# One set of five sigmoid buffers, V in three single-buffered tiles, one buffer for raw K, and four more weight tiles loaded during attention

## The chip, the cores and the metric

The kernel runs on one core of a Trainium2 chip. The metric is the device time of one execution in microseconds, the median of several runs. A core has a matrix engine (PE, whose weight loads are shown apart as PEld), a vector engine (DVE), an activation engine (ACT), a general engine (POOL) and a queue engine (SP); here SP issues every transfer. Transfers move between DRAM and the on-chip SBUF; matmuls write to PSUM. Each engine works through its own instructions in order and waits on semaphores that the others raise.

## The reference

Attention with a sigmoid in place of the softmax, and a "soft" mixture of experts on its output. Shapes: 8 batches, 12 heads, 448 positions, head size 64; 8 experts of 4 slots, model size 768, hidden size 1024.

```
scores = scale * q @ k.T - log(S)
attn   = sigmoid(scores);  x = attn @ v            # per batch and head
x      -> (3584, 768)
logits = x @ phi                                   # (3584, 32 slots)
slot_input = softmax over tokens(logits).T @ x     # (32, 768)
slot_out[e] = relu(slot_input[e] @ w1[e]) @ w2[e]  # per expert
out    = softmax over slots(logits) @ slot_out     # (3584, 768)
```

All inputs are float32. The weights w1 and w2 are 50 MB, q, k and v 33 MB, the output 11 MB.

## The kernel before, in words

The kernel has two stages that share the SBUF one after the other.

**Attention.** Two heads make a pair (128 partitions), and a loop takes two pairs, `pa` and `pb`, in each of 24 iterations (`NG`, three iterations to a batch). K's 448 positions are cut in three full chunks of 128 and a rest of 64, the "mid" chunk. One iteration issues on PE, in this order: `qk_full(pa)` and `qk_full(pb)` (scores, three chunks each), `av_full(pa)`, `av_full(pb)` (the product with V), the gate's `logits` of the iteration before, `qk_mid(n + 1)` (the mid scores of the next iteration) and `av_mid(n)`. ACT turns every chunk's scores into a sigmoid tile (`sigmoid`), six full ones and one mid per iteration. DVE copies the result out of PSUM (`evac`), transposes it (`turn`), and makes from the raw Q and K of the next two pairs the split float32r tiles `qs` and `ks` that `qk_full` reads (`split_all`, four DVE instructions per pair). SP loads Q and K of the next two pairs (`load_qk`), V of the next iteration (`load_v`), and a few weight units (`load_unit`).

From the fourth iteration on, the three iterations of a batch carry the gate's work for the batch before, and the code names them `edge` (n % 3 = 0), `after` (1) and `third` (2):

- edge: last logits between the two `av_full`, then `logits_add`, `softmax_a` and `softmax_b`.
- after: `softmax_r`, `softmax_c` and `spread`, which writes a tile to DRAM and reads it back four times (`zd`, `dr`); then, behind the splits, `logits` into PSUM buffer 3, `combine_b`, `logits_add`, and on PE `slot_job` ahead of `qk_mid`, which takes PSUM buffer 3 again.
- third: `slot_evac`, four `turn`s, `combine_c`; its `logits` are in PSUM buffer 0, which the next iteration's `qk_full` takes first.

The order on PE, SP, DVE and ACT is the order of the program's text (`manual_schedule`); semaphores come from the tiles: a new tile in a buffer waits until all readers of the old one are through. PSUM has four double buffers, `bank2(0)` to `bank2(3)`.

**Weights.** w1 and w2 are cut in 128 units of [128, 768] (384 KB). They go through a ring of `N_A + N_B` = 68 tiles: 47 `wa` tiles exist from the start and are filled during attention (`weights_of`: 3, 3, 3 units, then 4, 0, 3 per batch), and 21 `wb` tiles lie over the memory of the attention tiles and are filled as those come free, at the end of attention. Every later unit goes into the ring's next tile when its old unit has been used. The pools lie in SBUF in the order in which they are opened, and `wb0`, `wb1`, ... from the first attention pool upwards.

**Experts and output.** After the last softmax (`last_job`), `w1_part` and `w2_step` run through the units, and `out_batch` makes the output in 16 pieces of four stores each. The last 16 units (`N_LATE`) are mixed with the first 16 stores. Tiles of the output take places in the same ring.

## Time and profile before

| what | value |
|---|---|
| median of 3 runs | 391.66 us (391.07 to 392.79) |
| the profiled execution | 390.38 us, of which the span is 388.6 us |
| PE busy | 365.3 us, 94% of the span |
| DVE / ACT busy | 226.1 us (58%) / 187.5 us (48%) |
| bytes moved | 97.52 MB, mean 251 GB/s |
| attention | until about 283 us, then experts and output |

The profile cuts the span in 40 slices; a digit is the busy share of an engine in that slice in tenths. The view by stage gives the busy time of each engine between two times. The chain of waits follows the work that ended last back from its end: each step says which instruction or transfer held the next one. A name such as `PE b L182` is an engine, the tile that it writes and the line of the kernel; `SPq` is the queue engine issuing a transfer, `out<-in` its target and source. In the timeline, the first number of a row is its start and the second its duration; `[1.55 <-PE b L218]` is the idle time ahead of it and who ended it.

### The profile page before, as it was taken

The page shows a single profiled execution, that of the slowest core. Times are in us where ns is not written, and L with a number is a line of the kernel's source. Part 1 is how long each engine was busy: PE and PEld are TensorE (multiplying, and loading weights), DVE is VectorE, ACT ScalarE, POOL GpSimd, SP SyncE. Part 2 cuts the span into 40 slices and gives each one's busy share as a digit, 9 for nine tenths or more (in the row PEclk, how much of TensorE's full clock was granted, in tenths as well). Part 3 has the DMA queues.
Part 4 walks back from the last instruction along what each step waited for, and adds up shares of the span by engine and source line. Part 5 has one row for each costly group of instructions (what it writes and reads, how often), then busy time and mean ns, then how long its engine had stood idle before and what let it go on. Part 6 is the DMA issues. An engine that isn't in the chain of part 4 may idle for free.

```text
span 388.6 us, 9551 instructions
## 1 busy us (share of the span) xinstructions
PE 365.3 (94%) x3994; PEld 189.8 (49%) x3994; DVE 226.1 (58%) x518; ACT 187.5 (48%) x243; POOL 3.3 (1%) x13
## 2 busy tenths in 40 slices
PE   8999999999999999999999999999989989978760
PEld 7444556554555654555554455554455543224220
DVE  3655677775887677697767777776543410430250
ACT  5655676564567556566635666564531110320240
POOL 1000000000000000000000000000020000000000
PEclk9999999999999999999999999999999999999995
DMA  7766855662784567476446654323999999999997
GB/s 228 260 240 236 300 171 183 237 252 83 265 295 138 178 229 255 135 257 240 177 140 228 238 164 156 143 101 98 292 406 400 400 400 400 398 407 399 373 302 231
DMA packets 42363, 97.52 MB, mean 251 GB/s; under 512 B 4816, under 2 KB 16720, under 8 KB 42320
## 3 DMA queue, kind: packets, MB, share of 16 engines
q1 hardware_dynamic: 42320, 96.91, 70.3%
q8 instruction: 31, 0.51, 0.5%
q14 instruction: 12, 0.10, 0.1%
HBM read 85.43 MB, written 11.47 MB: 249 GB/s over the span
## 4 chain that ended last, share of the span: by engine, by line
PE 80%; DMA 14%; DVE 1%; SPq 1%; ACT 1%; issue 0%; ACTq 0%
PE b L189 29%; PE b L171 24%; DMA wa<-in_w_dram 8%; PE b L182 6%; DMA wb<-in_w_dram 6%; PE b L198 5%; PE b L312 4%; PE px L522 4%; PE b L218 3%; PE b L407 1%; PE px L565 1%; PE px L539 1%; SPq L579 1%; DMA out_dram<-wa 1%; DVE wa L570 0%
## 5 line engine op out<-in xcount | busy, mean ns | idle before, releaser
L161 ACT ACTIVATE att<-b,nbias 128x896 f32<-128x896 f32 x144 | 131.9, 1015 | 12.0 <-PE b L171 12.0
L189 PE MATMUL b<-att,v 128*64 128x448 f32 x576 | 115.3, 545 | 0.0
L171 PE MATMUL b<-qs,ks 64*128 64x448 f32 x864 | 95.9, 372 | 0.0
L171 PEld LDWEIGHTS b<-qs,ks 64*128 64x128 f32 x864 | 77.4, 184 | 26.6 <-PE b L182 11.3
L189 PEld LDWEIGHTS b<-att,v 128*64 128x64 f32 x576 | 38.5, 136 | 61.6 <-issue 50.2
L161 ACT ACTIVATE attm<-b,nbias 128x896 f32<-128x896 f32 x24 | 24.2, 1008 | 70.4 <-PE b L182 70.4
L207 DVE COPY xT<-b 128x896 f32<-128x896 f32 x23 | 25.1, 1092 | 32.7 <-PE b L198 32.7
L152 DVE TENSOR_TENSOR qs<-qkt,qs 128x448 fp32r<-128x448 f32 x48 | 30.0, 625 | 1.7
L152 DVE TENSOR_TENSOR ks<-qkt,ks 128x384 fp32r<-128x384 f32 x48 | 26.8, 558 | 1.6
L213 DVE STREAM_TRANSPOSE y<-xT 128x448 f32<-128x448 f32 x48 | 27.3, 617 | 0.4
L182 PE MATMUL b<-qkt 64*64 64x448 f32 x192 | 24.1, 570 | 0.0
L150 DVE CAST qs<-qkt 128x448 fp32r<-128x448 f32 x48 | 18.2, 380 | 8.8 <-DMA qkt<-in_qk_dram 7.7
L198 PE MATMUL b<-attm,v 64*64 64x448 f32 x192 | 22.4, 537 | 0.0
L570 DVE COPY wa<-px 96x768 f32<-96x768 f32 x13 | 12.2, 952 | 13.7 <-PE px L565 12.9
L570 ACT COPY wa<-px 128x768 f32<-128x768 f32 x13 | 10.3, 799 | 18.1 <-PE px L565 14.2
L565 PE MATMUL px<-st,lt_all 32*128 32x384 f32 (+1 forms) x128 | 16.7, 524 | 1.5 <-DVE st L601 0.7
L312 PE MATMUL b<-y,dr 32*32 32x192 f32 x896 | 17.7, 331 | 0.2 <-ACT dr L303 0.2
L218 PEld LDWEIGHTS b<-xT,phit 128*32 128x32 f32 x384 | 9.1, 109 | 17.0 <-issue 13.4
L522 PE MATMUL px<-wa,sT 128*32 128x256 f32 x282 | 16.8, 381 | 0.6 <-DVE sT L380 0.6
L150 DVE CAST ks<-qkt 128x384 fp32r<-128x384 f32 x47 | 16.6, 353 | 0.0
L218 PE MATMUL b<-xT,phit 128*32 128x96 f32 (+1 forms) x384 | 16.0, 266 | 0.2
L601 DVE COPY st<-px 128x384 f32<-128x384 f32 x2 | 1.1, 557 | 25.3 <-PE px L599 25.3
(132 smaller groups left out, 229.3 us busy)
## 6 DMA issues: line engine op xcount, KB each, us to landing
wa<-in_w_dram SPq DMA_DIRECT2D x92, 384.0 KB, 7.7
qkt<-in_qk_dram SPq DMA_DIRECT2D x48, 448.0 KB, 3.8
wb<-in_w_dram SPq DMA_DIRECT2D x36, 384.0 KB, 5.7
v<-in_v_dram SPq DMA_DIRECT2D x24, 448.0 KB, 5.7
out_dram<-wa SPq DMA_DIRECT2D x26, 192.0 KB, 3.3
out_dram<-wa SPq DMA_DIRECT2D x26, 144.0 KB, 3.3
dr<-zd SPq DMA_DIRECT2D x28, 64.0 KB, 2.0
out_dram<-wb SPq DMA_DIRECT2D x6, 192.0 KB, 5.5
```

The source lines that it names most:

```text
L150: copy(dst[:, 0, :], src)
L152: nc.vector.tensor_tensor(out=dst[:, 1, :], in0=src, in1=dst[:, 0, :].bitcast(F32), op=ALU.subtract)
L161: nc.scalar.activation(att[:], sc[:, :, 0:S], AF.Sigmoid, bias=nbias, scale=QSCALE)
L171: nc.tensor.matmul(sc[:, h, 0:S], ks[r, z, c * P:(c + 1) * P], qs[r, y, :], start=(z + y == 0), stop=(z == 1))
L182: nc.tensor.matmul(sc[r, h, 0:S], t[d, S + NQK:QW], t[d, 0:S], start=True, stop=True)
L189: nc.tensor.matmul(avs["p", p][r, 0:S], vs[n][:, i * (NFULL + 1) + c, r], atts[p, c][:, h, :], start=(start and c == 0), stop=(stop and c ...
L198: nc.tensor.matmul(avs["p", 2 * n + i][d, 0:S], vt[r, NFULL, d], att[r, h, :], start=start, stop=stop)
L207: nc.vector.tensor_copy(xTs[n][:], avs[n][:, :, 0:S])
L213: nc.vector.transpose(ys[b][:, hp, :], xTs["p", p])
L218: nc.tensor.matmul(lp[32 * j:32 * j + 32, 0:TOK[j]], phi_sb[:, p % NPR, :], xTs["p", p][:, TOF[j]:TOF[j] + TOK[j]], start=(first and m == ...
L312: nc.tensor.matmul(sl[a // 2][32 * j:32 * j + 32, a % 2, 0:NPR * BLK], drs[b][32 * a:32 * a + 32, j, c * BLK:(c + 1) * BLK], y[32 * a:32 * ...
L522: nc.tensor.matmul(ph[32 * j:32 * j + 32, uu, 0:256], sT[:, 3 * kh + kc, :], utile[("w1", e, 2 * uu + j // 2, kh)][:, kc * 256:(kc + 1) * ...
```

## The change

- The seven sigmoid tiles become five (`homes`): within an iteration the fifth and sixth sigmoid write over the first and second, the next mid one over the third, and the roles rotate from iteration to iteration.
- V of an iteration, before one tile in two buffers, becomes three tiles with one buffer each: `v0` and `v1` (the full chunks of pair a and of pair b) and `v2` (the mid chunks). `v0` and `v1` for the next iteration are loaded behind the weights; `v1` for a third iteration and every `v2` are loaded in the iteration that uses them.
- The load of Q and K is cut in two: Q with the mid K (`qkt`, two buffers, as before) and the full chunks of K (`kf`), for which there is one buffer for both pairs. The load for `pb + 2` comes behind `split_all(pa + 2)` in the program. Pair 1 alone uses the last weight tile's place. On the host the mid K is put ahead of the full K.
- In edge iterations the K part of `split_all(pb + 2)` goes behind `softmax_b`, and the logits there take PSUM buffer 3 in place of 0.
- Weight units are issued behind `split_all(pa + 2)` and the second K load in place of ahead of `qk_full(pa)`. 51 `wa` tiles and 17 `wb` tiles make the ring of 68.

```diff
@@ -25,12 +25,12 @@
 NFC = F // P
 HALF = DM // 2
 UNIT = 768
-N_A = 47
-N_B = 21
+N_A = 51
+N_B = 17
 N_LATE = 16
 N_MIX = 4
-NATT = 5
 QW = 2 * S
+QM = QW - NQK
 NP = B * NPR
 NG = B * NQ
 WARM = 8
@@ -116,9 +116,9 @@
     with ExitStack() as actx:
         ldq = actx.enter_context(tc.tile_pool(name="ldq", bufs=2))
         sp = actx.enter_context(tc.tile_pool(name="sp", bufs=2))
-        ata = actx.enter_context(tc.tile_pool(name="ata", bufs=1))
-        atb = actx.enter_context(tc.tile_pool(name="atb", bufs=1))
-        lvp = actx.enter_context(tc.tile_pool(name="lvp", bufs=2))
+        one = {}
+        for name in ("kf", "v0", "att4", "att3", "v2", "att0", "att1", "att2", "v1"):
+            one[name] = actx.enter_context(tc.tile_pool(name=f"{name}p", bufs=1))
         yp = actx.enter_context(tc.tile_pool(name="yp", bufs=1))
         xp = actx.enter_context(tc.tile_pool(name="xp", bufs=1))
         bounce = actx.enter_context(tc.tile_pool(name="bounce", bufs=2, space=bass.MemoryType.DRAM))
@@ -127,39 +127,47 @@
         def bank2(i):
             return ps.tile([P, 2, 512], F32, name=f"b{i}")
 
-        qkts, vs, splits, atts, avs, xTs, ys, dts, drs = {}, {}, {}, {}, {}, {}, {}, {}, {}
-
-        def load_qk(p):
+        kfs, qkts, vs, splits, atts, avs, xTs, ys, dts, drs = {}, {}, {}, {}, {}, {}, {}, {}, {}, {}
+
+        def load_qk(p, part=None):
             if p < NP:
-                t = ldq.tile([P, QW], F32, name="qkt")
-                nc.sync.dma_start(t[:], qk[p])
-                qkts[p] = t
-
-        def load_v(n):
+                if part != 1:
+                    qkts[p] = ldq.tile([P, QM], F32, name="qkt")
+                    nc.sync.dma_start(qkts[p][:], qk[p, :, 0:QM])
+                if part != 0:
+                    kfs[p] = (wpa.tile([P, UNIT], F32, name=f"wa{N_A - 1}")[:, 0:NQK] if p == 1
+                              else one["kf"].tile([P, NQK], F32, name="kf")[:])
+                    nc.sync.dma_start(kfs[p], qk[p, :, QM:QW])
+
+        def load_v(n, part):
             if n == NG:
                 return
-            vs[n] = lvp.tile([P, 2 * NFULL + 1, P], F32, name="v")
-            nc.sync.dma_start(vs[n][:], v[n])
+            lo, hi = ((0, NFULL), (NFULL + 1, 2 * NFULL + 1), (NFULL, NFULL + 1))[part]
+            vs[n, part] = one[f"v{part}"].tile([P, hi - lo, P], F32, name=f"v{part}")
+            nc.sync.dma_start(vs[n, part][:], v[n, :, lo * P:hi * P])
 
         def split(p, i, z, copy=nc.vector.tensor_copy):
             w = (S, NQK)[i]
             if z == 0:
                 splits[p, i] = sp.tile([P, 2, w], F32R, name=("qs", "ks")[i])
-            dst, src = splits[p, i], qkts[p][:, i * S:i * S + w]
+            dst, src = splits[p, i], kfs[p] if i else qkts[p][:, 0:S]
             if z == 0:
                 copy(dst[:, 0, :], src)
             else:
                 nc.vector.tensor_tensor(out=dst[:, 1, :], in0=src, in1=dst[:, 0, :].bitcast(F32), op=ALU.subtract)
 
-        def split_all(p):
+        def split_all(p, part=(0, 1)):
             if p < NP:
-                for i, z in ((0, 0), (0, 1), (1, 0), (1, 1)):
-                    split(p, i, z)
+                for i in part:
+                    split(p, i, 0)
+                    split(p, i, 1)
 
         def sigmoid(name, sc):
-            att = (atb if name == "att0" else ata).tile([P, 2, S], F32, name=name)
+            att = one[name].tile([P, 2, S], F32, name=name)
             nc.scalar.activation(att[:], sc[:, :, 0:S], AF.Sigmoid, bias=nbias, scale=QSCALE)
             return att
+
+        homes = [f"att{i}" for i in range(5)]
 
         def qk_full(p):
             qs, ks = splits[p, 0], splits[p, 1]
@@ -170,7 +178,7 @@
                     for h, r in enumerate(heads):
                         nc.tensor.matmul(
                             sc[:, h, 0:S], ks[r, z, c * P:(c + 1) * P], qs[r, y, :], start=(z + y == 0), stop=(z == 1))
-                atts[p, c] = sigmoid(f"att{u % NATT}", sc)
+                atts[p, c] = sigmoid(homes[u % 4], sc)
 
         def qk_mid(n):
             if n == NG:
@@ -179,23 +187,24 @@
             for i, r in enumerate(heads):
                 t = qkts[2 * n + i]
                 for h, d in enumerate(heads):
-                    nc.tensor.matmul(sc[r, h, 0:S], t[d, S + NQK:QW], t[d, 0:S], start=True, stop=True)
-            atts["mid", n] = sigmoid(f"attm{n % 2}", sc)
+                    nc.tensor.matmul(sc[r, h, 0:S], t[d, S:QM], t[d, 0:S], start=True, stop=True)
+            atts["mid", n] = sigmoid(homes[2], sc)
+            homes[:] = [homes[i] for i in (3, 0, 1, 4, 2)]
 
         def av_full(p, start, stop):
             n, i = divmod(p, 2)
             for c in range(NFULL):
                 for h, r in enumerate(heads):
                     nc.tensor.matmul(
-                        avs["p", p][r, 0:S], vs[n][:, i * (NFULL + 1) + c, r], atts[p, c][:, h, :],
+                        avs["p", p][r, 0:S], vs[n, i][:, c, r], atts[p, c][:, h, :],
                         start=(start and c == 0), stop=(stop and c == NFULL - 1))
 
         def av_mid(n, flags):
-            att, vt = atts["mid", n], vs[n]
+            att, vt = atts["mid", n], vs[n, 2]
             for h, d in enumerate(heads):
                 for i, r in enumerate(heads):
                     start, stop = flags[i]
-                    nc.tensor.matmul(avs["p", 2 * n + i][d, 0:S], vt[r, NFULL, d], att[r, h, :], start=start, stop=stop)
+                    nc.tensor.matmul(avs["p", 2 * n + i][d, 0:S], vt[r, 0, d], att[r, h, :], start=start, stop=stop)
 
         def new_x(n):
             xTs[n] = xp.tile([P, 2, S], F32, name="xT", bufs=2)
@@ -399,13 +408,14 @@
 
         load_qk(0)
         load_qk(1)
-        load_v(0)
+        load_v(0, 0)
+        load_v(0, 1)
         nc.sync.dma_start(csb[:], cst)
         nc.sync.dma_start(phi_sb, phi)
         pw = bank2(0)[:, 0, :]
         for _ in range(WARM):
             nc.tensor.matmul(pw[:, 0:WN], acc[:, 0:P], acc[:, 0:WN], start=True, stop=True)
-        dmy = ata.tile([P, 2, S], F32, name="attm0")
+        dmy = one["att2"].tile([P, 2, S], F32, name="att2")
         nc.scalar.activation(dmy[0:1, 0, 0:1], nbias[0:1, :], AF.Sigmoid)
         split(0, 0, 0)
         split(0, 1, 0, nc.scalar.copy)
@@ -419,8 +429,11 @@
             bp = n // NQ - 1
             edge, after, third = (n >= NQ and n % NQ == i for i in range(3))
             final = n == NG - 1
+            if third:
+                load_v(n, 1)
             load_qk(pa + 2)
-            load_qk(pb + 2)
+            load_qk(pb + 2, 0)
+            load_v(n, 2)
             if third:
                 slot_evac(bp)
             if n > 0:
@@ -431,9 +444,6 @@
                 softmax_r(bp)
                 softmax_c(bp)
                 spread(bp)
-            load_v(n + 1)
-            for _ in range(weights_of(n)):
-                load_unit()
             if third:
                 combine_c(bp)
             if edge and bp > 0 or final:
@@ -441,8 +451,16 @@
                 combine_d(bq, dts[bq][:, 0, 0:P])
             qk_full(pa)
             split_all(pa + 2)
+            load_qk(pb + 2, 1)
+            for _ in range(weights_of(n)):
+                load_unit()
+            load_v(n + 1, 0)
+            if not after:
+                load_v(n + 1, 1)
             qk_full(pb)
-            split_all(pb + 2)
+            split_all(pb + 2, (0,))
+            if not edge or final:
+                split_all(pb + 2, (1,))
             if final:
                 avs["p", pa] = bank2(2)[:, 0, :]
                 av_full(pa, True, False)
@@ -469,10 +487,11 @@
                 avs["p", pa + i] = avs[n][:, i, :]
             av_full(pa, True, False)
             if edge:
-                lp = logits(n - 1, 0)
+                lp = logits(n - 1, 3)
                 logits_add(lp, bp, False)
                 softmax_a(bp)
                 softmax_b(bp)
+                split_all(pb + 2, (1,))
             av_full(pb, True, False)
             if n > 0 and not edge:
                 lp = logits(n - 1, 3 if after else 0)
@@ -638,7 +657,7 @@
     q, k, v = inputs["q"], inputs["k"], inputs["v"]
     qT = q.transpose(0, 1, 3, 2).reshape(NP, P, S)
     kT = k.transpose(0, 1, 3, 2).reshape(NP, P, S)
-    qk = np.concatenate([qT, kT], axis=2)
+    qk = np.concatenate([qT, kT[:, :, NQK:], kT[:, :, 0:NQK]], axis=2)
     vp = v.reshape(NG, 2, 2, S, D)
     full = vp[:, :, :, 0:NQK].reshape(NG, 2, 2, NFULL, P, D).transpose(1, 0, 4, 3, 2, 5).reshape(2, NG, P, NFULL * P)
     mid = vp[:, :, :, NQK:].transpose(0, 1, 3, 2, 4).reshape(NG, P, P)
```

## Prediction, written before the changed kernel ran

> **What bounds the kernel now.** I read the page first, then the view by stage, the chain of waits, and the timelines of SP, DVE and PE in the seven "after" iterations and around the end of attention. The page (its rate in 40 slices of 9.7 us) and two stages:
>
> ```profile
> span 388.6 us, 9551 instructions
> ...
> GB/s 228 260 240 236 300 171 183 237 252 83 265 295 138 178 229 255 135 257 240 177 140 228 238 164 156 143 101 98 292 406 400 400 400 400 398 407 399 373 302 231
> ```
>
> ```profile
> 96.00:268.00 172.00, 172.00 (x1891) 92.67 (x1884) 127.37 (x305) 103.76 (x125) 0.00 (x0) 1.00 0.57 193
> ...
> 308.00:325.00 17.00, 15.79 (x216) 7.73 (x212) 2.74 (x7) 1.66 (x8) 0.00 (x0) 1.00 1.03 399
> ```
>
> There are two stages with two bounds. From 96 to 268 us PE is busy 172.00 of 172.00 us while the transfers use 57% of the DMA engines: attention is bound by PE, and any wait that PE gets there lengthens the kernel by itself. From the slice that ends at 291 us the rate stays near 400 GB/s, and the DMA engines are full (share 1.03): the experts are bound by the weight stream. A unit of 393,216 bytes at 399 GB/s takes 0.985 us. The change takes four units out of the second stage and puts new waits into the first.
>
> One "after" iteration and the next in the chain of waits (start, us, what), with the kernel's start:
>
> ```profile
> 4.96 1.42 PE b L182 x8
> ...
> 118.86 3.92 PE b L171 x36
> 122.78 4.66 PE b L189 x24
> 127.44 0.57 PE b L218 x14
> 128.02 2.12 PE b L312 x95
> 130.14 0.91 PE b L182 x8
> ...
> 135.72 4.66 PE b L189 x24
> ...
> 142.61 3.95 PE b L171 x36
> ```
>
> PE goes from qk_full to av_full, logits, slot_job, qk_mid without a gap. It leaves nothing to hide a wait behind.
>
> **The change part by part.**
>
> *The second K load in "after" iterations.* SP in that iteration, and SP and PE in the last one of the seven:
>
> ```profile
> 123.59 1.75 SPq L289 DMA_DIRECT2D dr<-zd  x4
> 125.44 0.38 SPq L142 DMA_DIRECT2D v<-in_v_dram  x1
> ...
> 265.48 0.37 SPq L142 DMA_DIRECT2D v<-in_v_dram  x1
> ```
>
> ```profile
> 269.10 0.98 PE L182 MATMUL b<-qkt 64*64 64x448 f32 x8
> ```
>
> and DVE's queue there:
>
> ```profile
> 124.70 0.35 DVE L150 CAST ks<-qkt 128x384 fp32r<-128x384 f32 x1
> 125.09 0.56 DVE L152 TENSOR_TENSOR ks<-qkt,ks 128x384 fp32r<-128x384 f32 x1
> 125.56 0.30 DVE L97 STREAM_TRANSPOSE t<-lt_all 128x128 f32<-128x128 f32 x1
> ...
> 126.22 0.29 DVE L101 TENSOR_TENSOR lt_all<-t,cm 128x128 f32<-128x128 f32 x1
> 128.07 0.56 DVE L227 COPY lt_all<-b 64x128 f32<-64x128 f32 x2 [1.55 <-PE b L218]
> ```
>
> Today both raw K come with Q ahead of the reloads, and DVE reaches ks of `pb + 2` at 124.70 without waiting. In the changed order the full K of `pb + 2` stands on SP behind `zd` and the four `dr`, where V stands now: it is issued at 125.44, and DVE waits for it. Queued on DVE behind that split are combine_b's three instructions and logits_add, and logits_add frees PSUM buffer 3, which qk_mid takes. From the landing: a semaphore hop (0.05, as from the logits' end at 127.44 + 0.57 to the copy at 128.07), cast to L97 0.86, L97 to L101's end 0.95, the two copies 0.56, a hop of 0.05: 2.47 us. PE wants qk_mid at 130.14, 4.7 us after the issue. So PE waits as soon as the load takes more than 2.2 us.
>
> No load of 192 KB alone is in the trace. Its neighbours (KB, us to landing): the V load at this very place, where the seven take 3.4 to 3.8; a weight unit with nothing ahead of it; and the reload `dr`:
>
> ```profile
> v<-in_v_dram SPq DMA_DIRECT2D x1, 448.0 KB, 3.4
> v<-in_v_dram SPq DMA_DIRECT2D x1, 448.0 KB, 3.8
> ...
> wb<-in_w_dram SPq DMA_DIRECT2D x1, 384.0 KB, 3.0
> ...
> dr<-zd SPq DMA_DIRECT2D x28, 64.0 KB, 2.0
> ```
>
> From V (mean 3.57) less 256 KB at 400 GB/s (0.66): 2.9. From `dr` plus 128 KB (0.33): 2.3. I take 2.8, nearer to V, which has the same place, the same source and the same four reloads ahead of it. Then logits_add ends at 125.44 + 2.8 + 2.47 = 130.71 and PE waits 0.57. Five of the seven iterations are like this one. In two (the last: 265.48 to 269.10) a reload's issue took longer, so that only 3.6 to 3.8 us lie between; the wait there would be 1.6, and as I don't know whether the slow issue recurs, I count them at 1.1. Sum 5 x 0.57 + 2 x 1.1 = **+5.0 us**. Bounds: with the reload's own 2.0 no wait in five and at most 0.9 in two, 0 to 1.7; with V's own 3.57 it is 5 x 1.34 + 2 x 2.4 = 11.5.
>
> The Trainium skill ("DMA: Bandwidth & Descriptors", Anatomy of one DMA) gives a transfer a fixed part of about 2.0 us plus bytes over 436 GB/s, and its rules say to coalesce small transfers. It speaks against cutting the loads, as each piece pays the fixed part again; for 192 KB it would give 2.45 us, waits of 0.2 (0.8 in the two), and about +2.6 in place of +5.0. The weight unit agrees with it (2.9 against 3.0); V behind the reloads does not (3.05 against 3.57).
>
> *The same load in the other iterations.* In a third one, DVE's ks split of `pa + 2` and the logits_add:
>
> ```profile
> 137.60 0.56 DVE L152 TENSOR_TENSOR ks<-qkt,ks 128x384 fp32r<-128x384 f32 x1
> ...
> 141.00 0.56 DVE L229 TENSOR_TENSOR lt_all<-b,lt_all 64x128 f32<-64x128 f32 x2 [1.02 <-PE b L218]
> ```
>
> The load is issued at 138.16, lands by 140.96, and logits_add is through 0.05 + 0.86 + 0.56 + 0.05 later, at 142.48; PE wants PSUM buffer 0 at 142.61. The margin is 0.1, so I book 0.3 for six such iterations; 0 if the load takes 2.6, 3.9 if 3.57. In edge iterations the ks split stands behind the softmax, where DVE has nothing else queued, and the new PSUM buffer is free: zero. The first K load of each iteration is asked for with Q as now; DVE comes to it later than it lands: zero.
>
> *V in single buffers.* `v0` can be issued when av_full(pa) is over (122.78 plus half of 4.66: 125.1) and is needed at 135.72: 10.6 us. Ahead of it lie at most four units (3.9) and its own 3.6, so 3 us are left; `v1` has the same distance. The mid V has most of an iteration. Zero; without that margin PE would wait from the first chunk on. SP issues four more loads per iteration at 0.4 each, at most 16 issues or 6.4 us of an iteration's 10.8 to 13: zero. Waits for av_full put the next Q load behind them, but av_full ends before the qk_mid that it waits for anyway.
>
> *Five sigmoid buffers.* The fifth sigmoid must wait for the first third of av_full(pa), over at 122.78 + 0.78 = 123.56; its reader, the second chunk of av_full(pb), comes at 125.11 + 0.78 = 125.89. That leaves 2.3 us for one ACT instruction: zero; without that slack each iteration would lose what is missing.
>
> *The start.* Q and mid K (256 KB each) land before 448 KB would; qk_mid takes 1.42 at the start against 0.91 elsewhere, so at most 0.5, and PE's warm-up ends at 4.96 anyway: **-0.3**.
>
> *Four units less in the tail.* They would save 4 x 0.985 = 3.9. But the tail has a gate:
>
> ```profile
> SPq L92 <- PE b L312: 1.9, 1, 1.9
> ```
>
> ```profile
> 287.80 0.33 SPq L92 DMA_DIRECT2D wb<-in_w_dram  x1
> ```
>
> ```profile
> wb<-in_w_dram SPq DMA_DIRECT2D x1, 384.0 KB, 6.0
> ```
>
> At 287.80 the unit that lies over the y tile is released by the last slot_mm (L312); it lands 6.0 us later because other units are still under way. It is number 47 + 17 = 64. The attention pools shrink by 12,288 bytes per partition (two sigmoid tiles 7,168, V 3,584, K 1,536), four units of 3,072, so after the change the first unit over y is number 51 + 13 = 64 as well. It can't be asked for before 287.80, and an undisturbed unit lands in 3.0: 290.8 in place of 293.8. The gain is at most 3.0; the stream runs nearly dry at this gate. Later the first store must wait for PE's out_batch, which doesn't move; I take 0.3 off. **-2.7**, between -3.9 (no gate) and -2.0 (a dry spell of 1 us).
>
> Sum: +5.0 + 0.3 - 0.3 - 2.7 = +2.3 on the profiled 390.38 (span 388.6 and 1.8 around it) gives 392.7. The median of the runs, 391.66, is 1.28 above that execution, so the time to be measured is 394.0.
>
> **The rivals.**
>
> *The load is quicker, and gain and loss cancel.* The unit's 3.0 for 384 KB and the reload's 2.0 for 64 KB give a line on which 192 KB take 2.4: waits of 0.17 in five and 0.7 in two, 2.3, none in the third ones, and 2.3 - 0.3 - 2.7 = -0.7: **391.0**. For it: nothing but the reloads is under way then. Against it: V at the same place is slower than that line.
>
> The skill's fixed part, above, would come out close to this case.
>
> *Attention keeps its pace, and the kernel is faster.* If the load takes under 2.2 us, logits_add is through before 130.14 and only the start and the tail are left: -3.0, **388.7**. For it: `dr` needs only 2.0. Against it: three times the bytes would have to land nearly as fast, from behind four reloads.
>
> *The load is as slow as V.* If the time is a wait for first data, with size of no weight, 3.57 holds: 11.5 + 3.9 - 3.0 = +12.4, **404**. For it: V in this place spends most of its time before data come at full rate. Against it: the undisturbed unit.
>
> *The tail gains nothing, since the stream is gated*: +5.3 - 0.3, **396.7**. Against it: the 6.0 us of the gated unit, which are queueing.
>
> **How the numbers follow.** About 0.5% (2.0 us) is what a measurement can tell from no change. The forecast (load of 2.6 to 3.1 us) has 0.47, of it 0.37 beyond +2.0 and 0.10 within; the cancelling rival 0.27, of it 0.23 within and 0.04 faster; attention at its pace 0.14, faster; the slow load 0.06 and the gated tail 0.06, both slower. Faster 0.18, same 0.33, slower 0.49. The likeliest case's own range is 392.5 to 397; the range goes down to 388.7, to hold the faster case, and up to 398.
>
> **What would show it.** Right: PE b L182 waiting for DVE lt_all L227 in the list of waits, seven times, about 0.6 each, and DVE ks L150 waiting for a transfer of kf just before; no such wait of L171 over 0.3. The first unit over y landing 3 us after its issue, the stream ending about 2.7 us nearer to attention's end. Wrong: PE still gapless there, with kf landing under 2.2 us; PE waiting for V or for a sigmoid; or the weight stream pausing longer at the gate than 1 us.

## The result, and the profile after

The changed kernel takes 412.08 us (median of six, 410.94 to 418.49) against 392.94 us for the kernel before, run beside it (six, 391.07 to 395.22): the ratio is 1.049, with an interval of 1.046 to 1.052. It is slower, as forecast, but by 19 us and not by 2. (Times are medians of all runs, ratios compare the fast runs alone; this kernel and those of 418.68 and 410.29 us below have one slow run each.) In the profiled execution the span is 411.0 us, 22.4 more than before. That is more than 19, as the profiled execution of the kernel before, 390.38 us, lies 2.6 below the median given here, and the one of the changed kernel 0.7 above it.

The code has moved down by some nine lines, so the names of the prediction become: qk_full L179, qk_mid L190, av_full L198, av_mid L207, logits L227, slot_job L321, the splits L155 and L157, the copies of logits_add L236; on SP Q L136, raw K L140, V L147, weight units L92, `zd` L295, `dr` L298. (In the experiments' kernels they can differ by some lines.)

The page of the changed kernel, its chain of what ended last:

```profile
span 411.0 us, 9759 instructions
...
PE 54%; DMA 28%; DVE 10%; SPq 3%; issue 2%; ACT 0%; DVEq 0%; ACTq 0%
PE b L198 18%; PE b L179 15%; DMA wa<-in_w_dram 10%; DMA zd<-t 6%; PE b L190 6%; DMA kf<-in_qk_dram 4%; DMA wb<-in_w_dram 4%; PE b L207 4%; PE px L541 4%; SPq L298 3%; PE b L227 2%; PE px L584 2%; DMA v<-in_v_dram 2%; DVE xT L216 2%; DVE t L268 1%
```

`kf`, the load that the prediction priced, is 4% of the chain. Ahead of it stands a transfer that the prediction gave no price: `zd`, the first write of spread (6%), and the issues of its four reloads (L298, 3%).

Iteration by iteration, from the first matmul of qk_full to the next: the seven "after" iterations are longer by 1.2, 3.1, 2.1, 5.3, 2.6, 3.0 and 2.1 us, 19.4 in all. The third iteration n = 8 is longer by 1.2, the start by 0.8, the tail behind the last slot matmul by 0.9, n = 18 by 0.3. Every other iteration is within 0.05 of before; these small steps sum to -0.3.

The list of waits after (total, times, longest), first PE and DVE, then SP's queue:

```profile
PE b L190 <- DVE lt_all L236: 10.9, 7, 1.9
PE b L198 <- DMA v<-in_v_dram: 2.4, 4, 0.9
DVE ks L155 <- DMA kf<-in_qk_dram: 36.3, 16, 4.9
DVE qs L155 <- DMA qkt<-in_qk_dram: 24.9, 15, 3.1
...
SPq L140 <- DMA kf<-in_qk_dram: 41.3, 16, 4.4
SPq L140 <- DVE qs L155: 39.0, 16, 4.1
SPq L298 <- DMA zd<-t: 21.3, 7, 3.8
```

and the last one's counterpart before:

```profile
SPq L289 <- DMA zd<-t: 8.2, 7, 1.2
```

The announced wait is there, qk_mid (L190) for logits_add, seven times; but 1.6 us each, not 0.6. Below it are the new ones. SP stands for the single K buffer (L140) for 80 us in all, and its wait for `zd` has gone from 1.2 to 3.0 us a time. DVE's Q splits wait for Q, 24.9 us.

SP's queue in the changed kernel, around the iteration that starts at 125.07 (the prediction's example, one iteration of PE after another, 118.79 before):

```profile
119.62 0.33 SPq L140 DMA_DIRECT2D kf<-in_qk_dram  x1
120.00 1.85 SPq L92 DMA_DIRECT2D wa<-in_w_dram  x4
121.90 1.94 SPq L147 DMA_DIRECT2D v<-in_v_dram  x2
124.42 0.33 SPq L136 DMA_DIRECT2D qkt<-in_qk_dram  x1
...
128.33 0.33 SPq L295 DMA_DIRECT2D zd<-t  x1
131.61 1.75 SPq L298 DMA_DIRECT2D dr<-zd  x4
133.46 0.38 SPq L140 DMA_DIRECT2D kf<-in_qk_dram  x1
```

and the same iteration in the chain of waits:

```profile
128.33 3.22 DMA zd<-t
...
133.46 2.50 DMA kf<-in_qk_dram
...
138.41 0.98 PE b L190 x8
```

Before, `zd` went out at the same point of the iteration (122.05, which is T + 3.26) and SP began `dr` 1.54 us later, at 123.59:

```profile
122.05 0.33 SPq L286 DMA_DIRECT2D zd<-t  x1
```

This is the reading that the case turns on. In the edge iteration SP stands at the second K load until DVE has split the first pair's K (119.62). Only then come the four weight units, both V loads and the next Q: 2.2 MB asked for between 120.0 and 124.8. At 128.33 `zd` is issued on time and waits behind them: 3.22 us to land, in which the DMA engines move 0.65 MB (203 GB/s, the last number of the first row below), ten times the 64 KB of `zd`. The second row is the last of the seven, which has no units ahead of it. (A row gives a stretch and its length, the busy time of PE, PEld, DVE, ACT and POOL, the granted clock, the DMA share and GB/s.)

```profile
128.33:131.55 3.22, 3.22 (x22) 1.45 (x20) 1.37 (x4) 2.84 (x4) 0.00 (x0) 1.00 0.57 203
280.56:283.59 3.03, 3.03 (x22) 1.31 (x20) 2.63 (x6) 2.65 (x4) 0.00 (x0) 1.00 0.11 30
```

It takes 3.03 us though the engines are nearly idle (share 0.11); the last section comes back to it. In the example, `dr` and the second K load, which SP issues behind it, go out 1.7 us late (133.46 is T + 8.39), the load itself takes 2.50, DVE's chain 2.45, and qk_mid starts at T + 13.34 in place of T + 11.35.

### The profile page after: what moved, and what is told of

It reads as the page before. It is cut to its first block, busy times and chain, and to the rows that moved or that the text cites. A ratio compares the mean times of both kernels' runs of the same rounds, so it can differ in the third digit from the quotient of the medians.

```text
span 411.0 us, 9759 instructions
## 1 busy us (share of the span) xinstructions
PE 372.4 (91%) x3994; PEld 194.0 (47%) x3994; DVE 228.0 (55%) x518; ACT 190.3 (46%) x243; POOL 3.3 (1%) x13
## 4 chain that ended last, share of the span: by engine, by line
PE 54%; DMA 28%; DVE 10%; SPq 3%; issue 2%; ACT 0%; DVEq 0%; ACTq 0%
PE b L198 18%; PE b L179 15%; DMA wa<-in_w_dram 10%; DMA zd<-t 6%; PE b L190 6%; DMA kf<-in_qk_dram 4%; DMA wb<-in_w_dram 4%; PE b L207 4%; PE px L541 4%; SPq L298 3%; PE b L227 2%; PE px L584 2%; DMA v<-in_v_dram 2%; DVE xT L216 2%; DVE t L268 1%
## 5 line engine op out<-in xcount | busy, mean ns | idle before, releaser
L167 ACT ACTIVATE att<-b,nbias 128x896 f32<-128x896 f32 x168 | 158.7, 1008 | 71.9 <-PE b L190 46.7
L198 PE MATMUL b<-att,v 128*64 128x448 f32 x576 | 115.3, 544 | 3.1 <-DMA v<-in_v_dram 2.4
L179 PE MATMUL b<-qs,ks 64*128 64x448 f32 x864 | 96.7, 375 | 0.0
L179 PEld LDWEIGHTS b<-qs,ks 64*128 64x128 f32 x864 | 78.7, 187 | 26.8 <-issue 6.9
L198 PEld LDWEIGHTS b<-att,v 128*64 128x64 f32 x576 | 40.0, 136 | 63.5 <-issue 53.1
L155 DVE CAST ks<-kf 128x384 fp32r<-128x384 f32 x46 | 16.4, 357 | 36.4 <-DMA kf<-in_qk_dram 36.3
L190 PE MATMUL b<-qkt 64*64 64x448 f32 x192 | 25.9, 583 | 10.9 <-DVE lt_all L236 10.9
L155 DVE CAST qs<-qkt 128x448 fp32r<-128x448 f32 x48 | 18.6, 388 | 27.6 <-DMA qkt<-in_qk_dram 24.9
L157 DVE TENSOR_TENSOR qs<-qkt,qs 128x448 fp32r<-128x448 f32 x48 | 30.0, 625 | 1.7
L157 DVE TENSOR_TENSOR ks<-kf,ks 128x384 fp32r<-128x384 f32 x47 | 26.2, 558 | 1.6
L207 PE MATMUL b<-att,v 64*64 64x448 f32 x192 | 23.7, 559 | 0.0
L283 ACT ACTIVATE t<-lt_all 128x128 f32<-128x128 f32 x7 | 2.2, 309 | 41.3 <-DVE lt_all L101 41.3
L321 PE MATMUL b<-y,dr 32*32 32x192 f32 x896 | 19.7, 332 | 1.4 <-DMA dr<-zd 1.2
L541 PE MATMUL px<-wa,sT 128*32 128x256 f32 x306 | 18.3, 381 | 0.6 <-DVE sT L389 0.6
L227 PEld LDWEIGHTS b<-xT,phit 128*32 128x32 f32 x384 | 9.1, 109 | 17.0 <-issue 11.3
L227 PE MATMUL b<-xT,phit 128*32 128x96 f32 (+1 forms) x384 | 16.0, 266 | 0.2
L190 PEld LDWEIGHTS b<-qkt 64*64 64x64 f32 x192 | 5.7, 135 | 21.8 <-issue 20.7
```

The lines of the kernel that those rows point to most:

```text
L155: copy(dst[:, 0, :], src)
L157: nc.vector.tensor_tensor(out=dst[:, 1, :], in0=src, in1=dst[:, 0, :].bitcast(F32), op=ALU.subtract)
L167: nc.scalar.activation(att[:], sc[:, :, 0:S], AF.Sigmoid, bias=nbias, scale=QSCALE)
L179: nc.tensor.matmul(sc[:, h, 0:S], ks[r, z, c * P:(c + 1) * P], qs[r, y, :], start=(z + y == 0), stop=(z == 1))
L190: nc.tensor.matmul(sc[r, h, 0:S], t[d, S:QM], t[d, 0:S], start=True, stop=True)
L198: nc.tensor.matmul(avs["p", p][r, 0:S], vs[n, i][:, c, r], atts[p, c][:, h, :], start=(start and c == 0), stop=(stop and c == NFULL - 1))
```

## The experiments

All are the changed kernel with the edit shown, or the kernel before with one. Times are medians; a ratio is to the kernel before on the same chip, with its interval.

**The two halves of the chain: the DVE order, and what is ahead of `zd`.** The first moves, in "after" iterations, the K split that waits for the late load behind logits_add:

```diff
-            if not edge or final:
+            if not (edge or after) or final:
                 split_all(pb + 2, (1,))
...
                 logits_add(lp, n // NQ, n % NQ == 1)
             if after:
+                split_all(pb + 2, (1,))
                 slot_job(bp)
```

> The changed kernel with one move: in after iterations the ks split of pb + 2 goes behind logits_add, so that DVE no longer holds logits_add, and with it PSUM buffer 3, while it waits for K. Theory A (PE loses its time to DVE waiting for K in front of logits_add): the seven waits of qk_mid for logits_add (10.9 us in all) go, and what is left is the late reload for slot_job, some 5 to 8 us, and V, 2 to 3: 398 to 403 us against 411. Theory B (PE loses its time to the single V and sigmoid buffers): no change, 409 to 412.

Measured: 401.31 us, 1.021 (1.018 to 1.025). The second puts the weight units back where they were, ahead of qk_full(pa) and so ahead of the second K load:

```diff
                 spread(bp)
+            for _ in range(weights_of(n)):
+                load_unit()
...
             load_qk(pb + 2, 1)
-            for _ in range(weights_of(n)):
-                load_unit()
```

> The changed kernel with one move: the weight units are issued where the kernel before has them, ahead of the second K load. Theory A says that the chain zd, dr, K is as late as it is since zd stands in the queue behind the units of the edge iteration: zd lands 1.5 to 2.5 us after its issue in place of 2.9 to 4.3, the second K load is issued 1 to 2 us earlier, and qk_mid waits 0.3 to 0.8 us seven times: 395 to 400 us. Theory B (the queue has nothing to do with it, V and sigmoid buffers hold PE): no change, 409 to 412.

Measured: 402.18 us, 1.021 (1.018 to 1.025), more than expected. The third has both edits.

> Both moves: the ks split of after iterations behind logits_add, and the weight units at their old place. Theory A: attention is back at the pace of the kernel before, and what is left is the tail with 0 to 2 us of gain and the start: 390 to 394 us, attention within 2 us of before. Theory B: 405 or more.

Measured: 396.92 us, 1.007 (1.003 to 1.011), again more than expected. From the lists of waits, first with the K split behind, then with the units early:

```profile
PE b L198 <- DMA v<-in_v_dram: 4.9, 6, 1.2
PE b L321 <- DMA dr<-zd: 1.6, 3, 0.6
SPq L298 <- DMA zd<-t: 22.5, 7, 3.8
```

```profile
PE b L190 <- DVE lt_all L236: 4.7, 5, 1.8
SPq L298 <- DMA zd<-t: 10.2, 7, 3.0
```

With the split behind, qk_mid no longer waits for DVE, but `zd` is as slow as ever (22.5 against 21.3 us of SP's waiting), so `dr` is late for slot_job and V for av_full: 10.5 us of attention's 21.5 remain. With the units early, `zd` lands in 1.52 to 1.54 us in six of seven iterations, and the waits of qk_mid fall from 10.9 to 4.7 us; but the units now push the K load back in the other iterations too (DVE's K splits wait 60.2 us for K, in the changed kernel 36.3), and four others are longer by 0.2 to 0.9: 11.6 us remain. Both together leave 4.6, of which 2.3 are in one iteration and 1.1 at the start. So the loss runs through both: a DVE queue that stops behind a late load, and a load that is late because of what SP holds up.

**Two K buffers.** The rest of the change stays, Q and K cut in two, V in three single tiles, five sigmoids; one of the late tiles fewer for want of room.

```diff
-N_A = 51
-N_B = 17
+N_A = 50
+N_B = 18
...
-            one[name] = ...(tc.tile_pool(name=f"{name}p", bufs=1))
+            one[name] = ...(tc.tile_pool(name=f"{name}p", bufs=2 if name == "kf" else 1))
...
-            load_qk(pb + 2, 0)
+            load_qk(pb + 2)
...
-            load_qk(pb + 2, 1)
```

> The changed kernel with two buffers for the full K and both K loads issued with Q at the start of the iteration (50 and 18 weight tiles in place of 51 and 17, to pay for the buffer). Everything else, the late units and the single V and sigmoid buffers too, stays. Theory A: DVE never waits for K behind the reloads, qk_mid does not wait, but zd is as late as in the changed kernel, so that slot_job waits for the reload: 397 to 403 us. Theory B: no change, 409 to 412.

Measured: 393.58 us, 1.002 (1.000 to 1.005), better than I had expected. Its SP waits:

```profile
SPq L139 <- DVE ks L156: 0.4, 1, 0.4
SPq L297 <- DMA zd<-t: 11.1, 7, 2.9
```

SP's 80 us of waiting for the K buffer have become 0.4. Attention is 1.2 us longer than before, 0.6 of it at the start. The units and V stand in their new place here too, but an SP that isn't held issues them early enough: `zd` lands in 1.5 to 1.9 us in six of seven iterations. The single K buffer, with the second load at the place that it forces on it, turns 1.002 into 1.049.

**The K part alone, on the kernel before.** One K buffer and the split loads, with the old V and seven sigmoids; the second K load behind the V load and the units, which stay where they were. The K part of the second split goes behind `softmax_b` in edge iterations, as in the change, but the logits there stay in PSUM buffer 0:

```diff
+                if part != 1:
+                    qkts[p] = ldq.tile([P, QM], F32, name="qkt")
...
+                              else kfp.tile([P, 2 * NQK], F32, name="kf"))[:, 0:NQK]
...
-            load_qk(pb + 2)
+            load_qk(pb + 2, 0)
...
             split_all(pa + 2)
+            load_qk(pb + 2, 1)
```

> The kernel before with the K part of the change alone: Q with the mid K in two buffers, the full K in one, its second load behind split_all(pa + 2), the ks split of edge iterations behind the softmax. V in two buffers, seven sigmoid buffers, 47 and 21 weight tiles; units and V are issued where the kernel before has them, ahead of the second K load. Theory A: the second K load stands behind zd and dr alone, zd lands 1.5 us after its issue, and qk_mid waits 0.3 to 1.5 us in seven iterations, 4 to 7 in all, which is the size that the prediction gave: 396 to 400 us. Rival B (single V and sigmoid buffers hold PE): 392 to 394, as before.

Measured: 418.68 us, 1.067 (1.059 to 1.074). And the same with V and the units behind that load, as in the change:

```diff
-            load_v(n + 1)
-            for _ in range(weights_of(n)):
-                load_unit()
...
             load_qk(pb + 2, 1)
+            load_v(n + 1)
+            for _ in range(weights_of(n)):
+                load_unit()
```

> The same with V and the weight units issued behind the second K load, as in the changed kernel. Theory A: SP waits for DVE's split of K before it issues them, so that they are still in the DMA queue when zd comes; zd lands 3 to 4 us after its issue and almost the whole loss is there without any other part of the change: 406 to 412 us. Rival: if the single V or the five sigmoid buffers are needed for the loss, it stays under 402.

Measured: 417.69 us, 1.065 (1.061 to 1.069). Both cost more than I had said. DMA issues of the first and of the second (KB, median us to landing):

```profile
kf<-in_qk_dram SPq DMA_DIRECT2D x47, 192.0 KB, 3.5
zd<-t SPq DMA_DIRECT2D x7, 64.0 KB, 1.5
```

```profile
kf<-in_qk_dram SPq DMA_DIRECT2D x47, 192.0 KB, 2.8
zd<-t SPq DMA_DIRECT2D x7, 64.0 KB, 4.1
```

The two pay in different places. With V and the units ahead, `zd` is undisturbed; K is issued at T + 7.4 to 8.5 and is slow (in the seven iterations 3.1 to 4.1 us). Third iterations are longer too, by up to 1.2. I had not counted the transfers that the K load would stand behind. With them behind it, K is quick, `zd` is the slow one, and but for 0.6 us in one third iteration only the "after" ones pay (1.5 to 6.0 us each), as in the change. The loss is complete without the V tiles and the five sigmoids; whether they cost something besides is asked next. It is also complete with `zd` undisturbed: the one K buffer costs by more than one path.

**The change without its K part.** Q and K whole in two buffers as before, V, sigmoids and late units as in the change, 50 and 18 tiles. To weigh what a unit loaded beside attention is worth, a second kernel has 47 and 21 tiles and 10,752 bytes per partition left unused ahead of y: the first unit over y is number 64 of the ring, as before (50 and 18 tiles: 63), and three units fewer are loaded beside attention.

```diff
-N_A = 50
-N_B = 18
+N_A = 47
+N_B = 21
...
+        gap = actx.enter_context(tc.tile_pool(name="gap", bufs=1))
+        gap.tile([P, 2688], F32, name="gap")
```

> The change without its K part: Q and K of the full chunks loaded whole in two buffers as before, and the five sigmoid buffers, V in three single tiles and the weight units beside attention as in the changed kernel; 50 of the late tiles ahead and 18 behind for want of room. Theory: the K buffer is the only part that costs, attention within 1 us of before, the tail gives at most 1.5 us: 390.5 to 393.5 us. Rival (V's single tiles or the sigmoids cost some 0.5 us for each of the seven iterations): 395 to 398 us.

> The kernel with K whole as in the run beside it, with 47 and 21 tiles and 10,752 bytes of a partition unused, so that the gate at the y tile stands three units earlier, as in the kernel before. Theory (three units at the gate are given back by the slow refill and by the stores): within 1 us of the run beside it. Rival (each unit at the gate is worth its transfer of 0.98 us): 2.5 to 3 us slower than it.

Measured: 393.75 us, 1.002 (0.999 to 1.005), and 393.62 us, 1.002 (1.000 to 1.004). Attention is 0.9 and 0.7 us longer than before in these profiles, nearly all of it in the start, one iteration and steps of 0.04. So nothing of V's single tiles, the sigmoids or the late units can be told from no change, in either direction. Three units more beside attention are worth nothing that can be measured here. The same pair on the kernel with two K buffers:

> The changed kernel with two K buffers, and 47 and 21 weight tiles in place of 50 and 18; unused memory ahead of the y tile keeps the last pools where the kernel before has them. Three units go back from attention to the tail. Theory G (the gate at the y tile, the slow start of the transfers after it and the first store, which waits for PE, take back what the units save): the same time as with 50 tiles, 392.5 to 394.5. Rival (the units are worth their bytes, 0.985 us each): 2.5 to 3 us slower, 395.5 to 397.

Measured: 394.63 us, 1.006 (1.003 to 1.009), against 393.58 us and 1.002 of its partner with 50 tiles. Three units by their bytes would be 3.0 us; the two pairs give none and about 1 (by their ratios 1.5, as the second pair ran on two chips). And the kernel before without the 16 units that are mixed with the stores (`N_LATE = 0`):

> The kernel before with no unit held back for the mixed part: all units are issued as ring tiles come free, all stores behind them. It asks what holds the end of the tail. If the wait of the first store for PE leaves the DMA engines idle, the stream is done earlier and the kernel gains 1 to 3 us: 390 to 392. If the queue is full over that wait, nothing, or a loss as the stores then are bound by their issue on SP: 392.5 to 395.

Measured: 393.78 us, 1.004 (1.002 to 1.006). The last unit lands 6 us earlier, 68.1 us after the last slot matmul in place of 74.4, and the end comes 2 us later in the profile: what the weights give back is lost again at the stores.

**The units away from `zd`.** Units in the "after" iterations in place of the edges, else the change:

```diff
-            share = 3 if n < NQ else (4, 0, 3)[n % NQ]
+            share = 3 if n < NQ else (0, 4, 3)[n % NQ]
```

> The changed kernel with the shares of the late weight units 0, 4, 3 in place of 4, 0, 3, so that none of them is issued in the edge between two pairs, ahead of the write of the decay factors (zd); the loads of Q, K and V still stand there. Theory A (the wait on the single K buffer holds SP, and what stood behind it runs into the write of zd): zd lands after 1.5 to 2.5 us instead of 2.9 to 4.3, the second K load is issued at T+6.6 to 7.6, the middle matmuls wait 0.6 to 1.5 us in each of seven iterations, 397 to 403 us. Rival (the late write is not a matter of the queue ahead of it): zd still 3 to 4 us, 409 to 412 us.

Measured: 410.29 us; its ratio, 1.037 (1.032 to 1.042), stands for 407 us. The step held and the sum did not. `zd` lands in 1.52 to 1.56 us in six of seven iterations, and the second K load is issued at T + 6.6 to 8.3. In the first four of the seven it goes out at T + 6.6 to 7.0, and qk_mid begins 0.2 to 0.6 us later than before: the size that the prediction gave. But two of these four iterations are longer by 2.5 and 6.5 us all the same, for there is a new stop. PE, one iteration:

```profile
171.72 0.98 PE L190 MATMUL b<-qkt 64*64 64x448 f32 x6 [0.25 <-DVE lt_all L236]
176.48 0.90 PE L190 MATMUL b<-qkt 64*64 64x448 f32 x1 [3.79 <-issue]
```

In the middle of qk_mid's eight matmuls PE stands for 3.79 us with no releaser. The transfers from 173.9 to 175.1 us by queue, and two stretches of time, in rows as above:

```profile
q1 hardware_dynamic: 268, 0.41, 100.9%
q8 instruction: 1, 0.02, 5.0%
```

```profile
172.70:176.40 3.70, 0.00 (x0) 0.00 (x0) 0.04 (x1) 0.00 (x0) 0.00 (x0) 0.84 0.85 306
176.40:179.80 3.40, 3.32 (x12) 1.00 (x13) 0.14 (x1) 1.01 (x1) 0.00 (x0) 0.50 0.20 50
```

One packet of the instruction queue, 16,384 bytes, moves on one DMA engine from 174.02 to 174.98, while the units fill all engines; PE goes on 1.5 us after its end. PE's two other stops without a releaser in attention, 1.74 and 0.68 us, end 1.3 and 1.5 us after such a packet too. There are 31 of them in the kernel, one for each 258 of PE's 7,988 instructions, and slot_job alone, with 112 matmuls and as many weight loads, uses up 224 in 2.2 us. I take it that PE ran out of instructions; the timing speaks for it, and no run isolates it. The Trainium skill ("Runtime: NRT & Kernel Launch", Instruction fetch mechanics) says that instructions come in blocks of 16 KiB, 256 of them, by the sequencer's own DMA queue, and that the cost is mostly hidden: the size and the count agree, and if that is what happened, it was not hidden in this run. The granted clock is 0.50 from 175.20, while PE still stands, and for 6.83 us.

**K from another queue.** The change with its second K load issued by POOL, in four parts:

```diff
+                    if part == 1:
+                        for r in range(0, P, 32):
+                            nc.gpsimd.dma_start(kfs[p][r:r + 32], qk[p, r:r + 32, QM:QW])
+                    else:
```

> The changed kernel, still with one K buffer, with the second K load of each iteration issued by POOL, as four transfers of 32 partitions, in place of SP; POOL has no other work in attention. Theory A (the buffer costs through SP, which stands still for it): units, V and the next Q go out at once, zd lands after 1.5 to 2.0 us, Q is there when DVE wants it (first split at T+3.2, where the changed kernel has T+5.0 to 6.1), no iteration but the seven is longer. In the seven the load starts when DVE has split K of pa+2, T+5.0, and the middle matmuls wait only for what it takes beyond 3.8 us: with 3 to 5 us for four pieces 0 to 1.2 us each, in all 392.5 to 402 us. Rival (one buffer costs the same whoever loads it): zd 3 to 4 us and 409 us or more.

Measured: 564.93 us, 1.44. `zd` is freed again (1.51 to 1.56 us in six of seven), as it should be if it was SP's standing still that delayed it; but the "after" iterations are 12 to 13 us longer here, time enough for any backlog to pass, so this run doesn't show it by itself. The load is far slower than I had allowed. POOL in the chain of waits:

```profile
163.52 0.50 POOL kf L142
164.02 2.72 issue
166.75 0.51 POOL kf L142
167.25 3.21 issue
170.46 0.51 POOL kf L142
```

The parts go out 2.4 to 3.7 us apart, and POOL waits for nothing that the profile shows in the stretches called issue; from the release, DVE's split that ends at 163.1, to DVE's next K split at 175.0 pass 11.9 us. DVE waits for K in 23 iterations. It says nothing of one buffer with a quick load; that wasn't tried.

## Why the prediction was wrong

**The second K load, +5.0: the mechanism right, the size 3.5 times too small.** Its place, its reader, the split ahead of logits_add on DVE, qk_mid as the one who pays: as written. From landing to qk_mid it gave 2.47 us; the seven show 2.45 to 2.46. The landing it took as 2.8; they show 2.36 to 3.24, mean 2.60. The Trainium skill's 2.45 ("DMA: Bandwidth & Descriptors", Anatomy of one DMA) is nearer, though that section's formula is for transfers issued by the general engine and these are issued by SP. The dearer guess from V was too high.

The step that failed is "it is issued at 125.44", T + 6.6. That is V's place in the old timeline, and everything ahead of it on SP was assumed to keep its time. But `zd`, two steps ahead of it, took 2.9 to 4.3 us to land in place of 1.5, in six of the seven behind what SP had held up. The load went out at T + 7.7 to 9.4, mean 8.75, where the prediction's sum has 6.8 on average (6.65 in five, some 7.2 in two). Those 1.95 us, less 0.2 for the quicker landing, are seven times 1.75 = 12.3: 5.0 became 17.3, and qk_mid does begin 17.5 us later in the seven together. Another 1.6 is the clock, below, in the one that is longer by 5.3 though its qk_mid came only 3.7 later; that leaves 0.3 of the 19.4.

**What hid it is a zero.** "SP issues four more loads per iteration at 0.4 each" counted SP's own time, and the first K load of an iteration and the edge were called zero since "DVE comes to it later than it lands". Nobody asked what stands behind SP's new wait: units, V and the next Q. The wait itself costs PE nothing in the edge; its price falls due in the next iteration, at `zd`. With the units early and with them elsewhere, `zd` is back at 1.5 us in six of seven, and the K load goes out at T + 6.6 to 7.0 in three and in four of them. Neither brings back the time; two K buffers do.

**Q, the second thing behind the wait.** DVE's splits were to begin at T + 3.15 as before. They begin at T + 5.04 in the example, as Q is late (24.9 us of waits), and the first K split, which frees the buffer, ends at T + 6.95. That is still ahead of the load's issue at T + 8.39, so it set nothing here. In the run with the units in the "after" iterations, where `zd` is on time, Q is on time too: the splits begin at T + 2.9 to 3.2 in all seven. So no run shows that this wait cost something of its own.

**Third iterations +0.3:** n = 8 is longer by 1.24, the rest by nothing. It isn't the load, but the clock. Two stretches of the changed kernel:

```profile
98.10:101.50 3.40, 1.48 (x24) 0.60 (x16) 2.94 (x8) 0.92 (x3) 0.00 (x0) 1.00 0.07 23
101.50:105.00 3.50, 3.50 (x20) 2.67 (x18) 2.84 (x5) 2.02 (x3) 0.00 (x0) 0.51 0.71 218
```

After 3.4 us in which PE was busy for 1.48, the granted clock is 0.51, and qk_full takes 5.16 us in place of 3.9. The Trainium skill ("TensorE: Matmul & The Clock Gate", The HAM clock gate) has half the clock follow an idle window of about 3.4 us: the length agrees, but here PE was 44% busy in the 3.4 us before, and an idle window wasn't needed. Nor is the busy time enough to tell: from 135.60 to 139.00 PE was busy for 1.61 of 3.40 us, and the clock stayed at 1.00. What decides it is open. So a wait can be paid twice.

**V and the sigmoids, zero: right in themselves.** V waits of 2.4 us came from SP's lateness; they are gone with two K buffers. The 3 us of room that was counted for `v0` held as long as SP was free.

**The start, -0.3:** +0.8 in this profile, 0.0 to +1.1 in the others that cut Q and K, and +0.4 in the run with `N_LATE = 0`, whose start is that of the kernel before. Pair 1's Q lands 1.2 us later than before, though fewer bytes stand ahead of it. Why wasn't settled.

**The tail, -2.7: measured +0.9.** The two kernels with the K part alone, whose ring and gate are those of the kernel before, show +0.9 and +1.1 in their profiles, so it can't be told from nothing. The gate is where it was put, and the unit over y lands 4.1 us after its issue, in place of 6.0 and against 3.0 forecast. The prediction saw a dry spell too, but only as a bound of 1 us, and at the gate alone. DMA share and GB/s (last two numbers) before and after the last slot matmul, kernel after, then before:

```profile
303.00:309.30 6.30, 5.84 (x158) 3.92 (x162) 2.97 (x11) 3.11 (x8) 0.31 (x1) 1.00 1.00 369
309.30:313.30 4.00, 3.42 (x55) 1.82 (x58) 1.81 (x7) 0.47 (x2) 1.86 (x7) 1.00 0.76 229
313.30:317.30 4.00, 4.00 (x72) 2.32 (x64) 0.75 (x1) 0.00 (x0) 0.00 (x0) 1.00 1.00 353
```

```profile
287.80:291.80 4.00, 3.42 (x54) 1.82 (x58) 1.81 (x7) 0.44 (x2) 1.86 (x7) 1.00 1.04 403
291.80:295.80 4.00, 4.00 (x72) 2.29 (x64) 0.75 (x1) 0.00 (x0) 0.00 (x0) 1.00 1.03 401
```

The stream falls to 229 GB/s for 4 us and is at 353 for the next four: 0.9 MB not moved, 2.2 us at 400 GB/s. The unit over y, number 64, has a lead of 1.9 us on before; number 70 has 0.2 left (11.7 us after the last slot matmul, before 11.9). At the stores it turns round: the last unit lands 75.6 us after it, before 74.4. The rival "the tail gains nothing" had the right number here, with 0.06; but the gated unit did land sooner, and what it gained was lost behind it.

**The rivals.** All let the second load go out where V did; the slow load changed only its duration. None has SP itself late, though the prediction quotes the queue in which `zd`, `dr` and the load follow each other. That is why 404 was the highest of them.

## What to carry to other kernels

A wait on an issuing queue isn't priced by who waits for that transfer, but by all that is queued behind it and by where that backlog will be in flight: look for the next small, urgent transfer, even in the next iteration. Going from two buffers to one moves the load's issue to its last reader; write the new issue time down from the release and the queue, don't take it from the place that another load had. Bytes taken out of a bandwidth-bound stage are worth what its gates let through; here, where a buffer's release starts the stream, filling the other buffers sooner only made it run dry.

## What the hardware showed that was not expected

- A 64 KB write lands in 1.52 us on a quiet queue, in 2.9 to 4.3 us behind some 2 MB asked for 4 to 8 us earlier. The last of the seven is another case: in the ten kernels, the changed one among them, in which it takes 2.2 to 3.5 us, a 16 KB packet of the instruction queue begins 0.1 to 1.5 us after its issue; in the four in which it takes 1.5, the kernel before among them, none moves meanwhile (by timing alone).
- The granted clock fell to 0.5 for 3.4 us after PE had been idle for 1.9 of 3.4 us, and qk_full took 5.16 in place of 3.9 us; after another stretch with 1.8 idle it did not fall.
- The weight stream, run nearly dry, moved 229 GB/s for 4 us and 353 for the next four, before it was back at 395.
- With the DMA engines full or nearly so, PE stopped for up to 3.8 us with no other releaser, each time until 1.3 to 1.5 us after an instruction packet of 16 KB (by timing alone).
- In the iteration shown, POOL issues transfers of 48 KB one after the other, 2.4 to 3.7 us apart; SP takes 0.4 us for one of 384 KB.
